# Two transformer layers on one core: units 1 and 2 transposed by DMA, room of the MLP lent to q and k, left-over projections laid by what is awaited

## The chip, the core and the metric

The kernel runs on one core of a Trainium2 chip. The core has five engines that work side by side, each through its own instructions in order: TensorE (PE, matmuls; its weight loads are listed apart as PEld), VectorE (DVE), ScalarE (ACT), GpSimd (POOL) and SyncE (SP). Here SP only issues DMAs; ACT issues the weight loads. All DMAs run on 16 DMA engines. Operands lie in SBUF with 128 partitions, matmul results in PSUM. An instruction waits on semaphores for what it needs, and everything behind it on its engine waits with it.

The metric is the device time of one execution in microseconds, lower is better. Before the change it is 1573.81 us (median of 3 runs, 1573.06 to 1575.74).

## The reference

Two layers over 2048 rows of 640 numbers. Each layer is sliding-window attention (32 heads of 20, a query sees itself and the 255 rows before it) and an MLP with a squared ReLU, both on layer-normalised rows, both added to the residual:

```python
def _A_ref(x, wqkv, wo):
    qkv = (x @ wqkv).reshape(B, S, 3, H, Dh).transpose(2, 0, 3, 1, 4)
    q, k, v = qkv[0], qkv[1], qkv[2]
    scores = jnp.einsum("bhqd,bhkd->bhqk", q, k) * (Dh ** -0.5)
    mask = (idx[:, None] - idx[None, :] >= 0) & (idx[:, None] - idx[None, :] < W)   # W = 256
    p = _softmax(jnp.where(mask, scores, -1e9))
    return jnp.einsum("bhqk,bhkd->bhqd", p, v).transpose(0, 2, 1, 3).reshape(B, S, D) @ wo

def _B_ref(x, w1, b1, w2, b2):
    r = jnp.maximum(x @ w1 + b1, 0)
    return (r * r) @ w2 + b2

x = x + _A_ref(_layernorm(x), wqkv, wo)
x = x + _B_ref(_layernorm(x), w1, b1, w2, b2)
# and both once more, with the same weights
```

## The kernel before

**Units and stages.** The work is cut into 16 units of 256 rows: eight for each layer, `u` from 0 to 15. A unit passes through these stages. Products are made from f16 pairs (a high half and the remainder as a low half) in three matmuls, so each projection below has three matmuls where the mathematics has one.

- The layernorm, then its rows transposed into `yT` (high and low halves). Units 0, 1 and 2 are transposed on TensorE (`ln_t`, which calls `split_t` at L382): ten 128x128 transposes a unit into PSUM, and from there copies on ScalarE (L389) and subtractions on VectorE (L390). Later units go through `ln_cross`: ScalarE casts a row block (L452), VectorE makes the low half (L456), and SP transposes both by DMA (L459), four transposes a unit.
- `stage_qk`: q and k, 75 matmuls each, in three pieces (two pieces of 30 and one of 15). A piece's PSUM bank is copied by ScalarE (the high half, L519) and then by VectorE (the low half, L522) into `qd`, and `leave` writes the rows to DRAM (L554, L556) and loads them back head by head (L560). Unit 0 does so piece by piece, later units after their third piece. `qd` is one buffer (`bufs=1`); k of unit 0 lies in the front half of `hraw` instead (the profile calls it `stg`), the space that later holds the MLP's `hh`.
- `stage_v`: v, 60 matmuls of 128x320, into one of six `vt` tiles.
- Attention in 8 quads a unit (four heads each). `max_quad` makes the scores once to find each row's maximum (`m`; L705 in unit 0 and 8, L673 elsewhere; VectorE reduces at L653 or L690). `max_out` turns the maxima of two quads by a transpose (`tr<-ident,mx`, L759) and `rows_out` sends them by DMA into two extra rows of q (`qt<-mT`, L727). `exp_quad` makes the scores again with the maximum subtracted (`s`; L856, L810), four exponentials on ScalarE (L795) and masks on GpSimd and VectorE; `pv_quad` multiplies by v (L901), and the result goes to DRAM (L921). The `m` of a quad runs three quads ahead of its `s` (`LEAD`). Both `m` and `s` write the same PSUM tiles `bb`, so each waits until the other's have been read.
- `load_o` fetches a unit's attention output, divides by the sums (L986, L989) and makes the pair `od` (L993, L996); `stage_o` multiplies by `wo` in two halves of 30 matmuls, adds the residual (L1025) and normalises again; `stage_y` (units 0 and 14, 15) transposes by TensorE, `y_cross` (others) by DMA; `stage_f` is the MLP, 180 matmuls into `hh` and 180 out of it.

All matmuls of projections and MLP rotate through two PSUM banks (tag `mm`), shared with `pv` and the transposes.

**What sets the order.** The program is laid out once, by a planner in the kernel's own code: `now` is its estimate of TensorE's time, and every job of another engine is posted with a cost, the jobs it depends on and an urgency (`post`, `dma`). When a job could start by `now` plus 250 ns it is put into its engine's program, the smallest number in `urgency` first. The costs decide only the order of instructions; at run time semaphores hold back what isn't ready. "Dense" work (projections, MLP) is a generator; while a quad's step waits for something by the planner's clock, the next piece of dense work is laid. `flow` does this for unit 0: its dense work is `ahead_all`, the projections of units 0, 1 and 2. What is left of it after unit 0's last quad is `rest`. `together` does it for units 1 to 15, with dense work of the unit before and the one after. For unit 1 the dense work is

```python
parts += [some(rest, left_over - 9e3), stage_o(0), some(rest, 4e3), stage_y(0, some(rest, 2e3), rest)]
```

where `some(rest, c)` lays about c ns of it. `KEEP` and `MID` say the same for the end of the program.

**Other tenants.** kts[2] (`kt_96`), the K tile of unit 2, first holds raw weights, then `yT` of unit 1 (`place`), then raw pieces of w2. `hraw` serves unit 0's k, and later `od` of unit 0 and `hh`; its second half lies idle during unit 0.

## Time and profile before

| | before |
|---|---|
| median of 3 runs | 1573.81 us |
| the profiled execution, whole | 1573.51 us |
| its span, first to last instruction | 1571.8 us |
| mean granted TensorE clock | 0.993 |
| TensorE idle after 162.57 us | 10.5 us |
| TensorE rows `tr<-ident,xt` (units 1 and 2, `y` of 0 and 14) | 40 of 286 ns each |

A row of the time view gives start and length in us, engine, source line, operation, `output<-input`, shape, and in brackets how long the engine stood idle before it and what ended that. A row of a group gives the busy time, the mean ns of one, and after the second bar the idle time before all of them. The duration of a single matmul (273 ns) holds its way through the array; in a row of them one starts every 0.11 to 0.15 us. "PEclk" is the share of full speed that TensorE's clock was granted. In the queue rows, "SPq" is a DMA issue on SP.

### The profile page before, as it was taken

The numbers are of one execution on the slowest core, as the hardware profiler recorded it, in microseconds if no ns is written. First come the engines' busy times: TensorE is split into PE (matmuls) and PEld (weight loads), VectorE is DVE, ScalarE is ACT, GpSimd is POOL, SyncE is SP. The second block draws the span as 40 slices with busy tenths as digits, with TensorE's granted clock in tenths as the row PEclk, the third lists the DMA queues.
The fourth block names the chain that finished last, engine by engine and source line by source line (L and its number), as shares of the span: only waits on it lengthen the run. The fifth ranks groups of instructions, "written<-read, shape, count | busy, mean of one in ns | idle before, by whom it ended". The sixth has DMA issues, their size and how long they took to land.

```text
span 1571.8 us, 58938 instructions
## 1 busy us (share of the span) xinstructions
PE 1541.4 (98%) x25842; PEld 1202.1 (76%) x25842; DVE 1041.4 (66%) x2248; ACT 669.1 (43%) x1369; POOL 453.6 (29%) x847
## 2 busy tenths in 40 slices
PE   8898999999999999999999999999999999999999
PEld 7565778777787877878777787877878778786777
DVE  8767775676756667666565756667676676667642
ACT  4554535345343443534434353344534434354422
POOL 1211414224141331413214142331513314132412
PEclk9999999999999999999999999999999999999999
DMA  9655244352433514354254433524344353432120
GB/s 277 173 166 151 63 124 92 91 130 60 115 97 103 115 51 125 88 120 97 72 134 81 116 97 104 113 54 123 88 126 90 71 133 74 118 89 59 30 68 18
DMA packets 243370, 160.86 MB, mean 102 GB/s; under 512 B 91176, under 2 KB 226856, under 8 KB 243112
## 3 DMA queue, kind: packets, MB, share of 16 engines
q1 hardware_dynamic: 236744, 147.58, 37.5%
q10 hardware_dynamic: 6368, 9.50, 2.1%
q8 instruction: 203, 3.33, 0.9%
q14 instruction: 55, 0.45, 0.1%
HBM read 84.68 MB, written 52.95 MB: 88 GB/s over the span
## 4 chain that ended last, share of the span: by engine, by line
PE 79%; DVE 7%; POOL 2%; issue 2%; ACT 1%; DMA 0%; SPq 0%; ACTq 0%; DVEq 0%; POOLq 0%
PE acc L339 61%; PE pv L901 6%; PE bb L810 5%; PE bb L673 4%; DVE mx L690 2%; PE bb L901 2%; POOL bmv L376 1%; POOL pt L824 1%; ACT pt L795 1%; DVE xt L378 1%; DVE bb L687 1%; DVE x L1128 0%; DVE bst L365 0%; DVE ot L916 0%; DVE bb L653 0%
## 5 line engine op out<-in xcount | busy, mean ns | idle before, releaser
L795 ACT ACTIVATE pt<-bb 128x640 f32<-128x640 f32 (+2 forms) x512 | 312.0, 684 | 210.9 <-PE bb L810 183.7
L824 POOL TENSOR_SCALAR_AFFINE_SELECT pt<-pt 64x256 f32<-64x256 f32 x448 | 195.4, 436 | 619.2 <-ACT pt L795 589.7
L339 PE MATMUL acc<-y,w_s 128*128 128x256 f16 x2880 | 328.9, 273 | 1.3 <-DVE y L390 1.2
L339 PE MATMUL acc<-w_s,hh 128*128 128x320 f16 (+1 forms) x2340 | 326.7, 297 | 0.1
L339 PEld LDWEIGHTS <-w_s 128*128 128x128 f16 x2880 | 275.5, 98 | 40.4 <-issue 2.3
L339 PEld LDWEIGHTS <-hh 128*128 128x128 f16 x2340 | 222.1, 98 | 86.8 <-issue 0.4
L690 DVE TENSOR_REDUCE mx<-bb 128x4 f32<-128x1024 f32 x224 | 274.0, 1223 | 6.2
L339 PE MATMUL acc<-yT,wq_s 128*128 128x256 f16 x2250 | 259.5, 273 | 3.5 <-DVE qd L522 2.5
L339 PEld LDWEIGHTS <-wq_s 128*128 128x128 f16 x2400 | 230.7, 98 | 41.2 <-issue 7.3
L833 DVE COPY_PREDICATED_SCALAR pt<-drop,zero 128x256 f32 x224 | 99.7, 498 | 178.9 <-ACT pt L795 178.2
L1099 DVE TENSOR_TENSOR hh<-r,hh 128x256 f16<-128x256 f32 x192 | 97.1, 519 | 112.1 <-ACT hh L1096 106.9
L901 PE MATMUL pv<-pt,vt 64*32 64x192 f32 (+5 forms) x3840 | 167.8, 304 | 0.5 <-POOL pt L867 0.3
L913 ACT COPY ot<-pv 128x256 f32<-128x256 f32 x128 | 47.6, 372 | 270.7 <-PE bb L901 244.3
L1093 POOL TENSOR_TENSOR r<-r 128x256 f32<-128x256 f32 x192 | 121.4, 652 | 136.1 <-ACT r L1089 133.4
L901 PE MATMUL bb<-pt,vt 64*32 64x64 f32 (+3 forms) x3584 | 153.9, 301 | 0.0
L901 PEld LDWEIGHTS pv<-pt,vt 64*32 64x32 f32 (+1 forms) x3840 | 126.0, 106 | 31.7 <-issue 3.7
L339 PE MATMUL acc<-wo_s,od 128*128 128x320 f16 x960 | 142.4, 303 | 5.8 <-ACT od L993 5.8
L339 PE MATMUL acc<-wq_s,yT 128*128 128x320 f16 x900 | 132.2, 302 | 1.3 <-DVE kt L390 0.5
L687 DVE COPY_PREDICATED bb<-maskq,bb 128x256 f32<-128x256 uint16 x224 | 93.8, 423 | 59.1 <-PE bb L673 56.6
L339 PEld LDWEIGHTS <-od 128*128 128x128 f16 x960 | 92.0, 99 | 45.8 <-ACT od L993 6.3
L1089 ACT ACTIVATE r<-acc,b1s 128x256 f32<-128x256 f32 x192 | 81.1, 476 | 96.0 <-PE acc L339 94.0
L901 PEld LDWEIGHTS bb<-pt,vt 64*32 64x32 f32 x3584 | 116.2, 106 | 0.4 <-DVE pt L833 0.2
(105 smaller groups left out, 1462.0 us busy)
## 6 DMA issues: line engine op xcount, KB each, us to landing
qt<-qk SPq DMA_DIRECT2D x30, 480.0 KB
kt<-qk SPq DMA_DIRECT2D x30, 480.0 KB
qk<-qd SPq DMA_DIRECT2D x17, 640.0 KB
o<-ot SPq DMA_DIRECT2D x256, 42.0 KB
od<-o SPq DMA_DIRECT2D x14, 640.0 KB
qk<-yl SPq DMA_DIRECT2D x13, 640.0 KB
qk<-qd SPq DMA_DIRECT2D x17, 320.0 KB
xt<-in_A_x_dram SPq DMA_DIRECT2D x16, 320.0 KB
```

The costliest lines, as they stand in the source:

```text
L339: nc.tensor.matmul(acc, lhs(a, c), rhs(b, c), start=(k == 0), stop=(k == 3 * nk - 1))
L673: nc.tensor.matmul(flat[e][rows, o:o + b - a], qt[r, p, i * P + 64 * h:i * P + 64 * (h + 1)], kt[r, p, a + to:b + to], start=True, stop=Tr ...
L687: nc.vector.copy_predicated(wins[:, :, 4 * Q:], later, wins[:, :, :Q])
L690: nc.vector.tensor_reduce(most, wins[:, :, Q:], axis=mybir.AxisListType.X, op=ALU.max)
L795: return lambda: nc.scalar.activation(room_of(box)[:, a:b], bank[:, a:b], AF.Exp, scale=SCALE / (QS * QS))
L810: nc.tensor.matmul(flat[e][h * Q:(h + 1) * Q, c0:c1], kt[r, 2 * qd + j, k0:k0 + Q], qt[r, 2 * qd + j, q:q + c1 - c0], start=True, stop=Tru ...
L824: nc.gpsimd.affine_select(out=m, in_=m, pattern=[[0, 4], [-1 if k else 1, Q]], base=0, fill=0.0, compare_op=ALU.is_gt if k else ALU.is_ge, ...
L833: nc.vector.copy_predicated(m, drop[:, k:k + 1, :].bitcast(mybir.dt.uint16).to_broadcast([P, 4, Q]), zero.unsqueeze(1).to_broadcast([P, 4, ...
L901: nc.tensor.matmul(pv[h][32 * jj:32 * (jj + 1), q0 * Q:(q0 + w) * Q], vf[r, c:c + 32], boxes[e]["pt"][r, a:b], start=(k == 0), stop=(k == ...
L1089: nc.scalar.activation(box["r"], acc[:, f, :], AF.Relu, bias=b1s[:, f0 + f:f0 + f + 1], scale=1.0 / (YS * WS))
L1093: nc.gpsimd.tensor_tensor(box["r"], box["r"], box["r"], op=ALU.mult)
L1099: nc.vector.tensor_sub(hh[:, 1, f, :], box["r"], hh[:, 0, f, :])
```

## The change

Four things change in the code.

1. Units 1 and 2 are transposed by DMA (`ln_early`, which calls `cross` as the later units do). The room for the casts is the second half of `hraw` ("side1").
2. k of units 0 and 1 is evicted into the front half of `hraw` ("side0"), q of unit 2 into the second ("side1"); k of unit 2 and the q of units 0 and 1 use `qd`. A record `left` keeps, for each of these buffers, which DRAM writes still read it, and the planner counts them as what the next tenant's copies depend on.
3. In unit 1 the left-over projections are laid by `until`: before `stage_o(0)` until the first two quarters of `od` are due by the planner's clock, before `stage_y` until the first block of `y` is, and between its two blocks until the second is.
4. Numbers of the planner: urgencies, the cost and landing time of the row DMAs, `KEEP` and `MID`.

```diff
-    urgency = {"out": 0, "od": 0.5, "cross": 2, "mask": 0, "turn": 1, "exp": 0.5, "ln": 1, "y": 1, "clear": 0.5}
+    urgency = {"out": 0, "od": 1, "cross": 1, "mask": 0, "turn": 1, "exp": 1, "ln": 1, "y": 0.5, "clear": 0.5}
...
+    def ln_early(u, place=None):
+
+        def dst():
+            yTs[u] = place
+            if place is None:
+                yTs[u] = sb.tile([P, 2, KC, T], F16, name="yT", tag="yT", bufs=1)
+            return yTs[u]
+
+        pre[u] = cross(lns.pop(u), dst, lambda: hraw[:, KC * T:2 * KC * T].bitcast(F16).rearrange(
+            "p (i a n) -> p i a n", i=2, a=2), 1)
+        left["side1"] = ((0, -u), pre[u], [])
...
-                if j and u == 0:
-                    qd = hraw[:, :KC * T].bitcast(F16).rearrange("p (c a n) -> p c a n", a=2, n=T)
+                if j and u < 2:
+                    qd, k = side(0), "side0"
+                elif u == 2 and not j and opened0:
+                    qd, k = side(1), "side1"
...
-                    qd = sb.tile([P, KC, 2, T], F16, name="qd", tag="qd", bufs=1)
+                    qd, k = sb.tile([P, KC, 2, T], F16, name="qd", tag="qd", bufs=1), "qd"
...
-                lo_ = post("D", 70 + 267 * n, low, post("A", 60 + 212 * n, high, wait=wait, prio=pr), prio=pr)
+                old = left.get(k, ())
+                if k and (j, u) != old[:1]:
+                    old = left[k] = ((j, u), [], old[1] if old else [])
+                hi_ = post("A", 60 + 212 * n, high, *(old[2] if k else ()), wait=wait, prio=pr)
+                lo_ = post("D", 70 + 267 * n, low, hi_, prio=pr)
...
+                if k:
+                    old[1].append(wrote)
...
-        return dma(spread, 16384, ready, n=4, cost=600.0, prio=0)
+        return dma(spread, 16384, ready, n=4, cost=650.0, prio=0, land=land)
...
+    def until(dense, jobs):
+
+        while not all(j.end is not None and j.end <= now[0] + LOOK for j in jobs()):
+            c = next(dense, None)
+            if c is None:
+                break
             yield c
...
-    QKC, VC, OC, FCST, LNC, CARRY, KEEP, MID = 16.4e3, 8.2e3, 8.2e3, 39.2e3, 1.2e3, 18e3, 28e3, 8e3
+    QKC, VC, OC, FCST, LNC, CARRY, KEEP, MID = 16.4e3, 8.2e3, 8.2e3, 39.2e3, 1.2e3, 18e3, 24e3, 10e3
...
         yield from stage_qk(0)
+        ln_early(1, place)
         yield from stage_v(0, range(2))
-        yield from ln_t(1, place)
         ln_load(2)
         yield from stage_v(0, range(2, 4))
+        ln_early(2)
         yield from stage_qk(1)
-        yield from ln_t(2)
         yield from stage_v(1)
...
-            urgency.update({"out": 0, "od": 1, "cross": 0.5, "mask": 0, "turn": 0.7, "exp": 0.5, "ln": 0.5, "y": 0.5, "clear": 0})
+            urgency.update({"out": 0, "od": 1.5, "cross": 1, "mask": 0, "turn": 0.7, "exp": 0.7, "ln": 0.5, "y": 1, "clear": 0.5})
...
-            parts += [some(rest, left_over - 9e3), stage_o(0), some(rest, 4e3), stage_y(0, some(rest, 2e3), rest)]
+            parts += [until(rest, lambda: ols[0][2][:2]), stage_o(0), until(rest, lambda: [ys[0, 0][1]]), stage_y(0, until(rest, lambda: [ys[0, 1][1]]), rest)]
```

Where the instructions stand is shown at three places; source lines differ by some 30 between the two programs, since the change adds lines.

ScalarE in the opening, from the third group of raw weights on (`kt_96`). `qd` and `stg` take q and k of unit 0 piece by piece, 128x2x256 is a piece of two, 128x256 the last. Before:

```order
L519 ACTIVATE qd<-acc 128x2x256
L271 ACTIVATE wq_s<-kt_96 128x5x128 x3
L519 ACTIVATE stg<-acc 128x2x256
L519 ACTIVATE qd<-acc 128x256
L519 ACTIVATE stg<-acc 128x256
L592 ACTIVATE vt_97<-acc 128x16x20
```

And of the changed kernel:

```order
L271 ACTIVATE wq_s<-kt_96 128x5x128 x3
L534 ACTIVATE qd<-acc 128x2x256
L534 ACTIVATE stg<-acc 128x2x256
L452 CAST stg<-xt 128x640
L300 DMA w_s<-in_A_wo_dram 32x5x640
L452 CAST stg<-xt 128x640
L534 ACTIVATE qd<-acc 128x256
L534 ACTIVATE stg<-acc 128x256
L622 ACTIVATE vt_97<-acc 128x16x20 x2
```

The weight conversions have moved ahead of q's second piece, and both casts of unit 1's rows ahead of the last pieces of q and k.

SP's queue right behind that, in the changed kernel: `kt_96<-stg` are unit 1's transposes, `yT<-stg` unit 2's, L583 and L585 the writes of q and k, L589 their loads by head, `qt<-mT` the first rows of maxima.

```order
L459 DMA_TRANSPOSE kt_96<-stg 128x5x128 x3
L589 DMA qt<-qk_0_267 60x6x256 x2
L589 DMA kt_94<-qk_1_310 60x6x256 x2
L583 DMA qk_0_267<-qd 128x512
L585 DMA qk_0_267<-qd 128x256
L583 DMA qk_1_310<-stg 128x512
L585 DMA qk_1_310<-stg 128x256
L459 DMA_TRANSPOSE kt_96<-stg 128x5x128
L430 DMA xt<-in_A_x_dram 128x640 x2
L757 DMA qt<-mT 1x8x128 x4
```

The eight transposes are new; before, the same loads and writes follow one another without them.

VectorE in unit 1 of the changed kernel, around the halves of `stage_o(0)`: `x_1539` is the residual of the first half, L1056 the addition of one `wo` bank, L365 to L370 the layernorm's statistics, L717 and L720 the reduction of a quad's maxima, L1027 the low half of a quarter of `od`, here the last.

```order
L1056 SCALAR_TENSOR_TENSOR x_1539<-acc,x_1539 128x320
L717 COPY_PREDICATED bb_143<-maskq,bb_143 128x4x64
L720 TENSOR_REDUCE mx<-bb_143 128x4
L1056 SCALAR_TENSOR_TENSOR x_1539<-acc,x_1539 128x320
L365 BN_STATS bst<-x_1539 128x6
L946 TENSOR_TENSOR ot<-bb_143,ot 128x256
L365 BN_STATS bst<-x_1539 128x6
L369 BN_AGGR bmv<-bst 128x2
L370 TENSOR_SCALAR bmv<-bmv 128x1
L1027 TENSOR_TENSOR od<-od 128x5x64
```

Before, the last quarter of `od` stands ahead of the first addition; now it stands behind both additions of the first half.

On TensorE the 20 transposes of units 1 and 2 are gone. Ahead of `stage_o(0)` all 60 v matmuls of unit 2 are laid now, and none is left for the places behind it; before, 60 of them stood between `stage_o(0)` and the MLP. Unit 0's last quad has the same projections ahead of it as before. From unit 1's seventh `m` (162.57 us in the profile of before) both orders lay the same matmuls, with a few of them moved over a neighbouring quad.

More of the change, by code (lines that the diff above doesn't have):

```diff
@@ L523, in low, with evict @@
                                                op0=ALU.mult, op1=ALU.subtract)
-            def evict(wait, n=n, c0=c0, high=high, low=low, jobs=jobs, j=j, dst=dst, qd=qd):
+            def evict(wait, k=k, n=n, c0=c0, high=high, low=low, jobs=jobs, j=j, dst=dst, qd=qd):
                 pr = urgency["out"]
-                lo_ = post("D", 70 + 267 * n, low, post("A", 60 + 212 * n, high, wait=wait, prio=pr), prio=pr)
+                old = left.get(k, ())
[3 more added lines that the diff above has]
+                lo_ = post("D", 70 + 267 * n, low, hi_, prio=pr)
                 jobs.append(lo_)
                 if u == 0:
-                    leave(u, j, dst, qd, lo_, c0, n)
+                    wrote = leave(u, j, dst, qd, lo_, c0, n)
                 elif c0 + n == KC:
-                    leave(u, j, dst, qd, lo_, 0, KC)
+                    wrote = leave(u, j, dst, qd, lo_, 0, KC)
+                else:
+                    return
+                if k:
+                    old[1].append(wrote)
             for c in range(n):
@@ L540, with side @@
     trips = {}
+    left = {}
+    opened0 = [True]
+    def side(k):
+        return hraw[:, k * KC * T:(k + 1) * KC * T].bitcast(F16).rearrange("p (c a n) -> p c a n", a=2, n=T)
     rows_of = {}
@@ L577, in leave @@
             load(*(rowset.get(u, ()) if j else ()))
+        return wrote
     def stage_v(u, which=range(4)):
@@ L719, with rows_out @@
     mxjobs = {}
-    def rows_out(qt, G, mT, ready):
+    def rows_out(qt, G, mT, ready, land=LAND):
         def spread():
@@ L941, in load_o @@
         l, g = divmod(u, NG)
+        opened0.clear()
         if late:
@@ L1179, in some @@
             yield c
+    def until(dense, jobs):
[3 more added lines that the diff above has]
+                break
+            yield c
     def portion(dense, cost):
@@ L1336 @@
             step(c)
-    left_over = 3 * (QKC + VC) + 2 * LNC - used[0]
+    left_over = 3 * (QKC + VC) - used[0]
     rate[0] = 320.0
```

7 lines of the change are left out of this document (4 added, 3 removed).

## The prediction

> **What bounds the kernel now.** I read the page first: span, busy shares and chain.
>
> ```profile
> span 1571.8 us, 58938 instructions
> PE 1541.4 (98%) x25842; PEld 1202.1 (76%) x25842; DVE 1041.4 (66%) x2248; ACT 669.1 (43%) x1369; POOL 453.6 (29%) x847
> PE 79%; DVE 7%; POOL 2%; issue 2%; ACT 1%; DMA 0%; SPq 0%; ACTq 0%; DVEq 0%; POOLq 0%
> ```
>
> TensorE is the bound: it is idle for 1571.8 - 1541.4 = 30.4 us. What an edit can win is idle time, time at the halved clock, and the few matmuls it takes away. So the second view is the busy time by stage. Columns: stretch, its length, then PE, PEld, DVE, ACT and POOL busy, granted clock, DMA share, GB/s.
>
> ```profile
> 27.87:47.70 19.83, 16.96 (x128) 11.32 (x126) 15.06 (x68) 4.22 (x10) 1.09 (x2) 0.91 0.94 224
> 47.70:112.67 64.97, 56.43 (x650) 39.55 (x650) 46.87 (x141) 37.03 (x78) 15.80 (x33) 0.96 0.61 174
> 112.67:162.57 49.90, 44.22 (x700) 31.97 (x697) 39.02 (x77) 23.48 (x47) 10.91 (x23) 0.91 0.49 130
> 162.57:1571.80 1409.23, 1398.73 (x24171) 1096.78 (x24170) 915.59 (x1905) 589.42 (x1211) 420.34 (x772) 1.00 0.38 93
> ```
>
> The stretches end where TensorE begins unit 0's v of its first half (27.87), its first scores for the exponentials (47.70), the work after its last `pv` (112.67), and unit 1's seventh maxima (162.57, from where both orders lay the same work). The first three hold 2.87 + 8.54 + 5.68 = 17.1 us of idle and, by their clocks, 1.8 + 2.6 + 4.5 = 8.9 us at half rate. The last, 1409 us long, holds 10.5 us. The change acts almost only ahead of 162.57, so **at most about 29 us** can go: 26 us, and 3 us of transposes.
>
> The third view is TensorE's rows in order of time (start, length; in brackets the idle time before and who ended it), and ScalarE's two that explain them.
>
> ```profile
> 27.87 3.29 PE L339 MATMUL acc<-wq_s,yT 128*128 128x320 f16 x23
> 32.48 0.49 PE L403 MATMUL tr<-ident,xt 128*128 128x128 f32 x3
> 36.05 4.42 PE L339 MATMUL acc<-wq_s,yT 128*128 128x320 f16 x19 [0.49 <-DVE kt L390]
> 47.70 0.49 PE L856 MATMUL bb<-qt,kt 62*128 62x256 f16 x7 [1.45 <-DMA qt<-mT]
> 66.24 3.69 PE L339 MATMUL acc<-kt,wq_s 128*128 128x256 f16 x20 [1.86 <-ACT ot L913]
> 79.37 1.25 PE L339 MATMUL acc<-wq_s,kt 128*128 128x320 f16 x8 [1.49 <-DVE yT L390]
> 109.80 0.71 PE L339 MATMUL acc<-yT,wq_s 128*128 128x256 f16 x5 [2.50 <-DVE qd L522]
> 126.36 7.04 PE L339 MATMUL acc<-wo_s,od 128*128 128x320 f16 x30 [3.81 <-ACT od L993]
> 65.32 0.60 ACT L519 ACTIVATE qd<-acc 128x512 f16<-128x512 f32 x1 [3.19 <-DMA qk<-qd]
> 108.42 0.60 ACT L519 ACTIVATE qd<-acc 128x512 f16<-128x512 f32 x1 [3.41 <-DMA qk<-qd]
> ```
>
> Three causes are to be seen: unit 2's transposes (79.37) and unit 1's (32.48 to 36.05); the single `qd` buffer, where k's first copy waits until q's rows have left (ScalarE at 65.32 and 108.42, so TensorE at 66.24, behind the same queue, and 109.80); and the attention output that isn't normalised when its projection comes (126.36).
>
> Holds cost twice. Same columns as above:
>
> ```profile
> 107.00:110.00 3.00, 0.50 (x6) 0.29 (x4) 1.20 (x4) 1.58 (x4) 0.41 (x1) 1.00 0.02 6
> 110.00:113.00 3.00, 3.00 (x61) 1.71 (x60) 2.55 (x6) 1.36 (x4) 1.90 (x3) 0.74 0.22 44
> 113.00:116.00 3.00, 3.00 (x21) 2.33 (x20) 2.97 (x5) 0.17 (x1) 0.00 (x0) 0.69 0.39 131
> 36.00:38.00 2.00, 1.95 (x9) 1.18 (x9) 2.00 (x14) 0.00 (x0) 0.00 (x0) 0.58 1.17 214
> 38.00:40.00 2.00, 2.00 (x10) 1.15 (x9) 0.87 (x6) 0.04 (x1) 0.00 (x0) 0.56 1.09 295
> ```
>
> After the 2.50 us hold the clock is 0.74 and 0.69 for 6 us, which is 1.7 us lost; after unit 1's transposes 0.58 and 0.56 for 4 us, 1.7 us again. I charge 1.7 us for each hold of 2 us and more. [...]
>
> **The change part by part: the opening, 27.87 to 47.70.** Removed are unit 1's ten transposes: between 32.48 and 36.05 TensorE spends 3.57 us, less 0.5 us for one quad's maxima: 3.1 us with their waits, and the 1.7 us of clock behind them. What comes in stands in the order on ScalarE: the copies of q's and k's last piece now stand behind both casts of unit 1's rows. (The new comparison sets a pair against a one-element tuple, so it never matches, and the planner puts each piece of unit 0 behind the last one's write.) TensorE's v of unit 0 needs the bank of q's last piece. The rows of before to lay it by:
>
> ```profile
> 24.98 0.49 DVE L365 BATCH_NORM_STATS2 bst<-xt 128x6 f32<-128x320 f32 x1
> 26.86 0.41 DVE L522 SCALAR_TENSOR_TENSOR qd<-acc,qd 128x256 f16<-128x256 f32 x1
> 30.83 0.61 DVE L378 TENSOR_SCALAR xt<-xt,bmv 128x640 f32<-128x640 f32 x1 [0.19 <-POOL bmv L376]
> L452 ACT CAST yl<-xt 128x640 f16<-128x640 f32 x52 | 38.0, 731 | 36.4 <-DVE xt L378 33.6 <-PE acc L339 2.3 <-ACT pt L795 0.5
> L456 DVE TENSOR_TENSOR yl<-xt,yl 128x640 f16<-128x640 f32 x52 | 42.6, 819 | 1.2 <-ACT yl L452 1.2
> ```
>
> Before, that bank was free at 26.86 + 0.41 = 27.3. Now the second `xt` ends at about 30.5 (its statistics, which start at 24.98 in the first row, stand one place further ahead, ahead of the third weight group), the cast (0.73) at 31.2, the piece's copy (0.4) at 31.6, the low halves behind the second L456 (0.82) at 32.2. TensorE, 0.9 us late by the conversions that moved ahead of q's second piece, stands from 28.8 to 32.2, then runs cold: 0.9 + 3.4 + 1.7 = 6.0 us against 4.8 us removed. The first scores wait for the row DMA as before (1.45 us); I lay them at 48.5 with 10 projection matmuls (1.15 us) fewer behind them: **2.0 us lost**.
>
> What TensorE no longer does, SP, ScalarE and VectorE do:
>
> ```profile
> L459 SPq DMA_TRANSPOSE yT<-yl x52: 1199/1227/2467, 192.5 to 1334.2; - x52
> L390 DVE TENSOR_TENSOR yT<-tr,yT 128x384 f16<-128x384 f32 (+1 forms) x4 | 1.9, 486 | 0.3 <-ACT yT L389 0.3
> ```
>
> Eight transposes take 8 x 1.23 = 9.8 us of SP's queue. Three of unit 1's stand ahead of the loads for quads 3 to 5, one ahead of unit 2's `xt` and of the first rows. I lay the fourth at 36.4 to 37.6 and its first reader at 43.5; a transpose lands within some 3 us, so it costs nothing while the queues keep up (if not: rival two). On VectorE four L456 replace eight L390, 3.3 against 3.7 us: nothing.
>
> **Unit 0's quads, 47.70 to 112.67.** Of 64.97 us, 8.54 are idle, 2.6 clock, 1.5 ten transposes: 52.4 us of work, now 53.5 with the 10 matmuls. k of unit 1 goes to `side0` and q of unit 2 to `side1`, both read out long before: the two `qd` waits go. What is late next is VectorE and ScalarE: VectorE's 46.87 us stand in 54 to 58 us instead of 65.
>
> ```profile
> L795 ACT ACTIVATE pt<-bb 128x640 f32<-128x640 f32 (+2 forms) x512 | 312.0, 684 | 210.9 <-PE bb L810 183.7 <-PE bb L856 15.5 <-DVE x L1128 3.5
> L690 DVE TENSOR_REDUCE mx<-bb 128x4 f32<-128x1024 f32 x224 | 274.0, 1223 | 6.2
> ```
>
> The maxima wait until ScalarE's four exponentials (0.4 to 0.7 us each) have left the banks, the next scores until VectorE's reductions (1.2 each) have. Laid quad by quad, five times the maxima stand 0.2 to 0.9 us, 2.8 us together, and a q or k copy that ScalarE puts between the exponentials takes 1.1 more: 3.9 us. So 57.4 us, to 105.9: **7.6 us won**.
>
> **Unit 1's first half, 112.67 to 162.57.** Of 49.90 us, 5.68 are idle, 4.5 clock: 39.7 us of work. The 3.81 us wait goes: with 40 q/k matmuls (0.115 us), 60 of v (3.29 / 23 = 0.143) and 3.9 us of scores and a `pv` ahead, `wo` comes 17 us after unit 0's last `pv`, and `od` was ready after 126.36 - 112.67 = 13.7. But then nothing is left: the order has no projection between `wo` and the MLP. Before, 60 of 0.14 us stood there, 8.6 us. What is late instead, laid by VectorE's order: the maxima behind the casts of `od` 1.1 us; `wo`'s second half behind both additions and the statistics 2.0; the second half's transposes behind its layernorm 2.3; the scores behind the reduction moved past it 1.4. The layernorm's price is read from before:
>
> ```profile
> 137.51 0.48 DVE L1025 SCALAR_TENSOR_TENSOR x<-acc,x 128x320 f32<-128x320 f32 x1
> 139.56 0.61 DVE L378 TENSOR_SCALAR xt<-x,bmv 128x640 f32<-128x640 f32 x1 [0.34 <-POOL bmv L376]
> ```
>
> 137.51 to 140.17 is 2.7 us, against 3 us of cover that VectorE's reductions share. Sum 6.8 us, and 1.7 for one cold stretch: 48.2, to 154.1: **1.7 us won**, more only if the chain runs through.
>
> **The rest, 1409 us:** the same matmuls. In each unit some 5 to 8 move over a quad, and one of four transposes changes place with the row maxima's: nothing, from -1 to +2 us. The other urgencies only choose that order.
>
> Sum: -2.0 + 7.6 + 1.7 = 7.3 won ahead of 162.57. The profiled execution took 1573.51 us, 0.3 below the median of 1573.81. **Forecast 1566.0** (7.3 to 7.8 won).
>
> **Rivals.** *One, the quads run through.* VectorE was busy for 72% of the second stretch, so it has room; without the 3.9 us, and with half of the 8.5 in the third, 1566 - 8 = 1558. For it: nearly no waits after 162.57 at 66%. Against: 82% here.
>
> *Two, unit 1's transposes land late.* From 36 to 40 us the DMA share is 1.17 and 1.09, and `wo`'s loads queue there.
>
> ```profile
> w_s<-in_A_wo_dram ACTq DMA_DIRECT2D x4, 400.0 KB
> ```
>
> 1.64 MB at the 214 and 295 GB/s of those rows are some 6.5 us. Were the fourth behind them, it would land at 47, not 41: 3.2 us of hold and 1.7 of clock, with the quads' waits doubled (3.9): 1575. [...]
>
> *Three, slower.* In every later unit the last transpose of `y` now stands behind the maxima's.
>
> ```profile
> 237.75 6.66 SPq L459 DMA_TRANSPOSE y<-yl  x4
> 244.96 1.13 SPq L747 DMA_TRANSPOSE mt<-mh  x1
> 252.56 4.00 PE L339 MATMUL acc<-y,w_s 128*128 128x256 f16 x35
> ```
>
> It would end at about 247.4, with 5.2 us to the MLP. If it landed later than that by 1.2 us in 13 units, 15.6 us would go: 1581.6. It decides from 0.8 us a unit on. Against it: transposes land in under 3 us.
>
> *Four, the left-over doesn't do what it is named for.* Two of the three new calls find nothing to lay; that is in the forecast at 6.8 us.
>
> **How the numbers follow.** Forecast, 1562 to 1570: 0.60. Rival one, 1555 to 1562: 0.13. Rival two, 1570.5 to 1576.5: 0.18. Rival three: 0.09. A measurement of this kernel tells about 0.2% (3.1 us) from no change, so faster is 0.73, same 0.18, slower 0.09. The range leaves out a third of rival one, a fifth of rival two and rival three: 1558 to 1575.5.
>
> **What would show it.** In the changed profile: a hold of 3 us and more ahead of the first `acc<-wq_s,yT`, ended by VectorE's `qd`; no ScalarE wait for `qk<-qd`; `wo` without a hold at its first half and holds of about 2 us at its second and at the last `tr`; the seventh maxima of unit 1 near 154. It is wrong if the first `kt,wq_s` matmul of unit 1 waits for a DMA, or if the stretch behind gains or loses over 2 us.

## The result, and the profile after

The changed kernel takes **1561.38 us** (median of 4 runs, 1560.94 to 1563.26), before 1574.57 on the same chip (1573.06 to 1575.74): a ratio of 0.9919, 95% interval 0.9902 to 0.9936. It is faster by 13 us, and the forecast was 7.8: the time lies 0.6 us below the band of 1562 to 1570 that the forecast had for itself, and in the band of rival one.

The page of the changed kernel, span and busy time:

```profile
span 1559.6 us, 58897 instructions
PE 1533.5 (98%) x25822; PEld 1198.6 (77%) x25822; DVE 1043.3 (67%) x2244; ACT 669.7 (43%) x1365; POOL 451.8 (29%) x847
```

TensorE's idle time is 1559.6 - 1533.5 = 26.1 us, 30.4 before. The same stretches as in the prediction (length, PE, PEld, DVE, ACT, POOL busy, clock, DMA share, GB/s), in the changed kernel:

```profile
28.88:48.14 19.26, 14.34 (x108) 9.19 (x107) 14.79 (x66) 3.32 (x8) 2.02 (x2) 0.91 0.86 189
48.14:104.05 55.91, 53.94 (x649) 38.69 (x650) 41.26 (x126) 34.24 (x72) 14.60 (x33) 1.00 0.87 217
104.05:152.36 48.31, 43.47 (x698) 32.29 (x696) 40.60 (x80) 25.47 (x50) 14.54 (x23) 0.93 0.57 148
152.36:1559.60 1407.24, 1396.00 (x24171) 1095.42 (x24170) 921.01 (x1910) 591.53 (x1213) 415.15 (x772) 1.00 0.38 93
```

TensorE goes on with unit 0's first scores at 48.14 (47.70 before), unit 0's last `pv` is done at 104.05 (112.67), unit 1's seventh maxima begin at 152.36 (162.57), and the rest takes 1407.24 us (1409.23). So -0.4, +9.1, +1.6 and +2.0 us: 12.2 in all.

The same 12.2 us by kind. In both profiles half clock comes in steps of 3.41 us, each worth 1.71: six before (36.3, 67.1, 111.4, two from 125.1, and 1452.9 us), three after (34.2, two from 140.1), 5.1 us. Idle time is 4.3 us less. The 2.7 us that are left are about what the twenty transposes took.

TensorE's rows of the changed kernel that answer to those of the prediction:

```profile
33.06 0.70 PE L339 MATMUL acc<-wq_s,yT 128*128 128x320 f16 x4 [4.18 <-DVE qd L537]
47.61 0.27 PE L886 MATMUL bb<-qt,kt 62*128 62x256 f16 x1 [0.36 <-DMA qt<-mT]
101.48 0.71 PE L339 MATMUL acc<-yT,wq_s 128*128 128x256 f16 x5 [0.64 <-DVE qd L537]
129.86 0.75 PE L840 MATMUL bb<-qt,kt 62*64 62x128 f16 x37 [1.34 <-DVE ot L946]
140.24 1.30 PE L403 MATMUL tr<-ident,xt 128*128 128x128 f32 x5 [1.78 <-DVE xt L378]
1441.23 0.97 PE L339 MATMUL acc<-wo_s,od 128*128 128x320 f16 x4 [1.97 <-ACT od L1024]
```

The opening hold is there (4.18 us), the waits for `qk<-qd` and the 3.81 us ahead of `wo` are gone, the chain behind `y`'s layernorm is short of cover as laid. The hold of 1.97 us near the end is the same as before, row for row.

### The profile page after: what moved, and what is told of

It reads as the page before. It is cut to its first block, busy times and chain, and to the rows that moved or that the text cites. A ratio compares the mean times of both kernels' runs of the same rounds, so it can differ in the third digit from the quotient of the medians.

```text
span 1559.6 us, 58897 instructions
## 1 busy us (share of the span) xinstructions
PE 1533.5 (98%) x25822; PEld 1198.6 (77%) x25822; DVE 1043.3 (67%) x2244; ACT 669.7 (43%) x1365; POOL 451.8 (29%) x847
## 5 line engine op out<-in xcount | busy, mean ns | idle before, releaser
L854 POOL TENSOR_SCALAR_AFFINE_SELECT pt<-pt 64x256 f32<-64x256 f32 x448 | 199.3, 445 | 582.1 <-ACT pt L825 560.0
L720 DVE TENSOR_REDUCE mx<-bb 128x4 f32<-128x1024 f32 x224 | 273.2, 1224 | 6.8
L943 ACT COPY ot<-pv 128x256 f32<-128x256 f32 x128 | 47.6, 372 | 276.1 <-PE bb L931 247.2
L931 PE MATMUL bb<-pt,vt 64*32 64x128 f32 (+3 forms) x3584 | 153.5, 301 | 0.0
L717 DVE COPY_PREDICATED bb<-maskq,bb 128x256 f32<-128x256 uint16 x224 | 93.8, 423 | 85.7 <-PE bb L703 80.0
L339 PEld LDWEIGHTS <-yT 128*128 128x128 f16 x900 | 87.1, 98 | 40.0 <-issue 6.2
```

The source lines that it names most:

```text
L339: nc.tensor.matmul(acc, lhs(a, c), rhs(b, c), start=(k == 0), stop=(k == 3 * nk - 1))
L717: nc.vector.copy_predicated(wins[:, :, 4 * Q:], later, wins[:, :, :Q])
L720: nc.vector.tensor_reduce(most, wins[:, :, Q:], axis=mybir.AxisListType.X, op=ALU.max)
L854: nc.gpsimd.affine_select(out=m, in_=m, pattern=[[0, 4], [-1 if k else 1, Q]], base=0, fill=0.0, compare_op=ALU.is_gt if k else ALU.is_ge, ...
L931: nc.tensor.matmul(pv[h][32 * jj:32 * (jj + 1), q0 * Q:(q0 + w) * Q], vf[r, c:c + 32], boxes[e]["pt"][r, a:b], start=(k == 0), stop=(k == ...
L943: nc.scalar.copy(ot[:, qd % 2], to)
```

## The experiments

Each kernel is the changed one with an edit, unless said; the two named "alone" are the kernel before with one. Runs were taken on several chips, the kernel before beside each; its median there is 1573.67 to 1574.57 us. "To unit 1's wo" is the time from the start to the first matmul of unit 1's product with `wo`, with TensorE's idle time in it (its length less TensorE's busy time) and the number of steps at half clock. Behind it all fourteen profiles take 1343 to 1349 us, and up to it 212 to 232 us, so that most of the differences arise ahead of it.

| kernel | median us | ratio to before (95%) | to unit 1's wo | idle | half-clock steps |
|---|---|---|---|---|---|
| before | 1574 | 1 | 224.3 | 19.9 | 5 |
| changed | 1561.38 | 0.9919 (0.9902 to 0.9936) | 214.1 | 14.8 | 3 |
| e0_again | 1560.22 | 0.9912 (0.9899 to 0.9925) | 212.8 | 15.8 | 2 |
| e1_compare | 1575.75 | 1.0012 (1.0002 to 1.0022) | 230.2 | 24.6 | 7 |
| e2_one_qd | 1562.30 | 0.9923 (0.9910 to 0.9935) | 215.2 | 17.9 | 3 |
| e3_turn_on_pe | 1576.57 | 1.0016 (1.0005 to 1.0026) | 230.5 | 23.9 | 7 |
| e4_some | 1569.85 | 0.9971 (0.9961 to 0.9981) | 221.2 | 21.0 | 5 |
| e5_old_numbers | 1571.87 | 0.9989 (0.9979 to 1.0000) | 223.6 | 20.9 | 7 |
| e6_blind | 1565.15 | 0.9944 (0.9927 to 0.9961) | 218.1 | 17.1 | 5 |
| f1_early_alone | 1582.75 | 1.0055 (1.0039 to 1.0071) | 231.7 | 26.8 | 7 |
| f2_rooms_alone | 1568.80 | 0.9969 (0.9957 to 0.9980) | 220.6 | 19.8 | 2 |
| e7_swap | 1561.72 | 0.9922 (0.9908 to 0.9937) | 217.7 | 17.8 | 4 |
| e8_od_first | 1558.95 | 0.9901 (0.9885 to 0.9918) | 213.2 | 16.1 | 2 |
| e9_warm | 1556.52 | 0.9887 (0.9872 to 0.9902) | 212.4 | 12.0 | 2 |

### The changed kernel again

No edit.

> The changed kernel once more, unaltered, as the mark for the others. Time 1561.4 us within 1.5. What it is to tell besides: in both first profiles TensorE stands 1.97 us ahead of the same projection of the last units (acc<-wo_s,od, ended by ScalarE's od), but only before the change 3.4 us at the halved clock follow. Theory: the halved clock comes in steps of a grid of 3.41 us (every start of such a stretch in one trace is a multiple of 3.413 us from the others), and a hold costs clock when enough of it falls into one step; where the grid lies differs from execution to execution. Then the hold of 1.97 us is there again and may or may not be followed by 3.4 us of half clock, which is 1.7 us of time either way, while the holds near 29 to 33 us and 137 to 142 us are cold again or move by a step. Rival: the end of the changed kernel is laid better; then no such stretch after 150 us in any execution of it.

Measured: 1560.22 us. The hold near the end is there, with 1.96 us, and no half clock follows. The opening hold, 4.18 us again, cost two steps here and one in the first profile; the chain behind `y` cost two there and none here, with nearly the same holds. So where half clock falls differs between executions of one program, and part of every difference below 3.4 us can be that.

In both first profiles the hold near the end is the same, and only before the change half clock follows it. The window view, the step that holds it and the step behind, before:

```profile
1449.45:1452.86 3.41, 1.45 (x44) 0.91 (x43) 2.57 (x8) 2.48 (x5) 0.93 (x3) 1.00 0.20 55
1452.86:1456.28 3.42, 3.42 (x74) 1.98 (x80) 2.85 (x6) 0.36 (x1) 1.52 (x3) 0.50 0.00 0
```

and of the changed kernel, by the grid on which its own half-clock steps lie (from 34.25 and from 140.06 us, 31 steps of 3.413 us apart):

```profile
1437.13:1440.54 3.41, 2.14 (x48) 1.26 (x46) 2.33 (x6) 1.60 (x3) 0.18 (x1) 1.00 0.19 52
1440.54:1443.96 3.42, 2.65 (x105) 1.84 (x106) 2.63 (x8) 1.24 (x3) 2.27 (x5) 1.00 0.02 3
```

Before, the whole hold lies in one step (TensorE busy 1.45 of 3.41 us) and the next step runs at 0.50. After, it is cut into 1.27 and 0.69. Twelve traces have this hold, 1.96 to 1.97 us each: in four (before, e2, e7, f2) it lies whole in one step, and half clock follows; in eight the larger part is 1.03 to 1.71 us, and it never does.

### The comparison set right

```diff
-                if k and (j, u) != old[:1]:
+                if k and (not old or (j, u) != old[0]):
```

> The comparison in the eviction of q and k set right (a pair against the recorded pair), nothing else. ScalarE's copies of unit 0's last pieces then stand ahead of the casts of unit 1's rows. Theory (the order of ScalarE is the whole cause of the 4.18 us that TensorE stands from 28.88 us on): the hold falls below 0.7 us, the half clock at 34.2 us goes, and the time falls by 4 to 5.5 us against the changed kernel, to about 1556.5. Rival (what the first scores for the exponentials wait for is the rows of the maxima, made by VectorE and a DMA, not TensorE): they start at 46.5 us or later with a hold of 1.5 us and more ahead of them, and the time falls by 1.5 us or less. A second rival: the casts, now later, make unit 1's transposed rows late, with a hold of over 1 us ahead of unit 1's first q or k matmuls.

Measured: 15.5 us slower than e0. The opening hold is gone, and another stands 19 us later. ScalarE's rows; the second has the shortest, median and longest time of one of its issues of `wo` in ns:

```profile
38.14 7.56 ACTq L300 DMA_DIRECT2D w_s<-in_A_wo_dram  x3
L300 ACTq DMA_DIRECT2D w_s<-in_A_wo_dram x4: 567/572/717, 38.1 to 49.2; - x4
45.91 0.60 ACT L534 ACTIVATE qd<-acc 128x512 f16<-128x512 f32 x1 [8.15 <-DMA w_s<-in_A_wo_dram]
51.26 0.60 ACT L534 ACTIVATE qd<-acc 128x512 f16<-128x512 f32 x1 [4.75 <-DMA xt<-in_A_x_dram]
```

and TensorE's, there and later:

```profile
51.94 0.80 PE L339 MATMUL acc<-kt,wq_s 128*128 128x256 f16 x3 [5.40 <-DVE qd L537]
139.29 0.27 PE L703 MATMUL bb<-kt,qt 60*64 60x256 f16 x1 [2.26 <-ACT pt L825]
185.50 0.75 PE L703 MATMUL bb<-kt,qt 60*64 60x128 f16 x24 [1.80 <-DMA kt<-qk]
213.01 0.37 PE L703 MATMUL bb<-kt,qt 60*64 60x256 f16 x1 [2.13 <-ACT pt L825]
```

In the new order ScalarE issues three loads of `wo` in a row, and q of unit 1 is copied behind them. The 7.56 us aren't three slow issues, since none takes over 0.72 us. The trace's semaphores tell what ScalarE waits for: the third issue (45.14) waits until the DMA that last used its semaphore has landed. That is a load of q which SP issued at 38.58, complete at 45.12, so ScalarE stands 5.3 us between the second issue (39.25 to 39.83) and the third. The DMA engines are 97% busy from 38 to 46 us; that this made the load slow fits, but wasn't tried apart. Two further weight loads, issued at 49.21 and 50.80, wait in the same way, each for a load of `xt`, and the copy at 51.26 stands behind them. Later, at 185.50, unit 2's first maxima wait for k: its load was issued at 177.62 us (161.68 in the changed kernel), because the tile holds raw pieces of `w2` until VectorE's last conversion (172.54 against 157.36). All of this comes from one comparison in the eviction: the planner's clock shifts and everything behind is laid differently. **So undoing a part in the planner doesn't price that part.** None of the expected outcomes had that size.

### One qd

```diff
-                if j and u < 2:
+                if j and u == 0:
...
-                elif u == 2 and not j and opened0:
-                    qd, k = side(1), "side1"
```

> k of unit 1 and q of unit 2 go to the one buffer qd again, all else as in the changed kernel. Theory (the single buffer's waits were what was won in unit 0's quads): ScalarE waits for the DMA of qk<-qd some 3 us twice, TensorE 1.9 and 2.5 us behind it, with up to 1.7 us of half clock for each: 4.4 to 7.8 us slower than the changed kernel. Rival (VectorE and ScalarE bind the quads anyway): the waits come back on ScalarE but TensorE's holds are covered, 2 us slower or less.

Measured: 1562.30 us, 2 us above e0 with intervals that overlap. That is the rival's size, but not its cause, as the next run shows: the planner, which now knows of the waits, lays other work there. TensorE's longest two holds there are 1.27 us at 101.19 and 1.09 us at 103.67.

### One qd, and the planner not told

As above, and

```diff
-                hi_ = post("A", 60 + 212 * n, high, *(old[2] if k else ()), wait=wait, prio=pr)
+                hi_ = post("A", 60 + 212 * n, high, *(old[2] if k and u == 0 else ()), wait=wait, prio=pr)
```

> As with one qd for k of unit 1 and q of unit 2 (1562.3 us), and besides the planner isn't told that the copies of units 1 and 2 wait for the DMA that reads the buffer, as it wasn't before the change. Theory (what replaced the waits of 1.86 and 2.50 us is that the planner knows of them and lays other work there, not the second buffer): ScalarE stands 3 us for qk<-qd again with other work behind it, TensorE 1.5 to 2.5 us at one or two places between 60 and 115 us, 2 to 6 us slower than with one qd. Rival (those waits were a consequence of the transposes on TensorE, or are covered): within 1.5 us of the run with one qd.

Each engine's order is here that of the changed kernel, only the buffers differ: this is the price of the rooms alone. Measured: 1565.15 us, 4.9 above e0, 3.8 above the first run of the changed kernel and 2.9 above one qd. ScalarE and TensorE:

```profile
102.75 0.60 ACT L532 ACTIVATE qd<-acc 128x512 f16<-128x512 f32 x1 [2.99 <-DMA qk<-qd]
```

```profile
104.12 1.22 PE L339 MATMUL acc<-yT,wq_s 128*128 128x256 f16 x5 [2.70 <-DVE qd L535]
```

2.70 us against 0.64 in the changed kernel (101.48 us there), and two half-clock steps from 103.09 us: 2.1 + 3.4 = 5.5. The theory holds, at one place of two.

### The rooms alone, on the kernel before

```diff
-                if j and u == 0:
+                if j and u < 2:
                     qd = hraw[:, :KC * T].bitcast(F16).rearrange("p (c a n) -> p c a n", a=2, n=T)
+                elif u == 2 and not j and opened0:
+                    qd = hraw[:, KC * T:2 * KC * T].bitcast(F16).rearrange("p (c a n) -> p c a n", a=2, n=T)
```

> The kernel before, with k of unit 1 and q of unit 2 in the two halves of the MLP's room and nothing else: every engine's order is that of before, only the buffers differ. Theory (the prediction's: the two waits for qk<-qd go, with their half clock): TensorE's holds of 1.86 us at 66 us and 2.50 us at 110 us go, 4.4 to 7.8 us faster than before, 1566 to 1569.5. Rival (something else is late there at once): the holds shrink, but what comes out is less than 2 us faster.

Again no instruction moves. Measured: 1568.80 us, ratio 0.9969, 5 us faster than before. The holds of 1.86 and 2.50 us are gone or down to

```profile
104.52 0.71 PE L339 MATMUL acc<-yT,wq_s 128*128 128x256 f16 x5 [0.64 <-DVE qd L524]
120.59 0.45 PE L339 MATMUL acc<-wo_s,od 128*128 128x320 f16 x2 [3.81 <-ACT od L997]
130.38 0.28 PE L762 MATMUL tr<-ident,mx 128*16 128x128 f32 x1 [2.73 <-DVE x L1029]
```

and of the gain some goes into a new hold of 2.73 us at 130.38. The two runs agree: **the rooms are worth about 5 us**, at either end of the change (4 to 5 by the one, 3 to 7 by the interval of the other).

### The transposes, undone and alone

Undone:

```diff
-        ln_early(1, place)
         yield from stage_v(0, range(2))
+        yield from ln_t(1, place)
...
-        ln_early(2)
         yield from stage_qk(1)
+        yield from ln_t(2)
```

> Units 1 and 2 are transposed on TensorE again, in their old places, all else as in the changed kernel. Twenty transposes are 2.7 us of TensorE (busy time less what half clock cost, before against after). Theory (by the steps of the prediction): in the opening the hold of 4.18 us goes, and the transposes with their waits of 0.2 to 0.7 us and one half-clock stretch come instead, 0.4 to 2 us in favour of TensorE's transposes; in the quads the transposes of unit 2 and their waits (0.8, 0.2 and 1.5 us) cost 4 us: in sum 2 to 4 us slower than the changed kernel. Rival (the transposes by DMA pay at both places): 6 us slower or more. Second rival (they pay at none): no slower.

Alone, on the kernel before: `ln_early`, the reverse of these lines, and the estimate `left_over` without the transposes' cost.

> The kernel before with the transposes of units 1 and 2 by DMA alone: no buffers, no record, no new rule, no new numbers. Theory (the transposes carry the gain, as the undoing of them cost 15 us and that of the buffers 1 to 2): the twenty transposes (2.7 us), their holds (3.9 us) and their half clock (1.7 us) go, 5 to 8 us faster than before, 1566 to 1569, with the qk<-qd waits still there. Rival (the parts only work together, since each alone shifts the planner's order and w2's conversions): within 3 us of before or slower, and unit 2's k is loaded after 166 us.

Measured: undone 16 us slower than e0, alone 9 us slower than before. Both theories fall: undone, the first rival's 6 us and more came, and alone, the rival. Undone, TensorE's transposes stand for VectorE:

```profile
40.37 0.77 PE L403 MATMUL tr<-ident,xt 128*128 128x128 f32 x5 [3.20 <-DVE kt L390]
81.18 1.30 PE L403 MATMUL tr<-ident,xt 128*128 128x128 f32 x5 [3.77 <-DVE xt L378]
```

Alone, other holds come:

```profile
51.04 0.37 PE L867 MATMUL bb<-qt,kt 62*128 62x256 f16 x1 [3.00 <-DVE bst L365]
66.64 0.60 PE L339 MATMUL acc<-kt,wq_s 128*128 128x256 f16 x4 [3.32 <-DVE qd L533]
194.55 0.75 PE L684 MATMUL bb<-kt,qt 60*64 60x128 f16 x20 [2.65 <-DMA kt<-qk]
```

Unit 2's k is loaded at 168.3 us undone and at 185.9 us alone. The edit's own price can't be read from either run, since the whole order behind it differs: what the transposes alone are worth isn't shown.

### Left-over by amounts

```diff
-            parts += [until(rest, lambda: ols[0][2][:2]), stage_o(0), until(rest, lambda: [ys[0, 0][1]]), stage_y(0, until(rest, lambda: [ys[0, 1][1]]), rest)]
+            parts += [some(rest, left_over - 9e3), stage_o(0), some(rest, 4e3), stage_y(0, some(rest, 2e3), rest)]
```

> The left-over projections of unit 1 are laid by amounts again (9 us kept back ahead of the first product with wo, 4 us and 2 us behind it), all else as in the changed kernel. Theory (the prediction's step): the product with wo stands some 3.8 us for od again, with up to 3.4 us of half clock, and in exchange the holds behind y's layernorm (1.34, 0.64, 1.78 and 0.36 us, with 3.4 to 6.8 us of half clock) become shorter: within 2 us of the changed kernel, 1559 to 1563. Rival (the new rule is where unit 1's first half was won): 4 us slower or more. Second rival, from the two runs that were 15 us slower: whatever leaves projections behind the first wo moves the conversions of w2 back, so that the load of unit 2's k (kt<-qk, issued at 161.7 us in the changed kernel, 177.6 and 168.3 us in those two) comes after 166 us, and 6 to 15 us go behind 150 us.

Measured: 9.6 us slower than e0: the first rival. Nearly all of it lies ahead of the first `wo` (124.69 us, 123.39 in e0): up to there TensorE has been idle for 17.2 us (11.0 in e0), with four steps at half clock (two in e0). (Unit 2's k is loaded at 166.65 us, and nothing waits for it.) Up to 108 us the order is that of the changed kernel, so this place can be read. Groups of TensorE's matmuls from 108 to 125 us here (count, busy time, mean, idle time before):

```profile
L703 PE MATMUL bb<-kt,qt 60*64 60x64 f16 (+3 forms) x76 | 3.2, 305 | 4.9 <-ACT pt L825 4.9
L840 PE MATMUL bb<-qt,kt 62*64 62x64 f16 (+3 forms) x76 | 1.7, 222 | 2.1 <-DVE mx L720 2.1
L339 PE MATMUL acc<-wo_s,od 128*128 128x320 f16 x2 | 0.5, 342 | 0.0
L339 PE MATMUL acc<-yT,wq_s 128*128 128x256 f16 x1 | 0.3, 273 | 0.0
```

and from 106 to 122.5 us in the changed kernel:

```profile
L339 PE MATMUL acc<-wq_s,yT 128*128 128x320 f16 x60 | 8.8, 299 | 0.3 <-DVE mT L795 0.3
L339 PE MATMUL acc<-yT,wq_s 128*128 128x256 f16 x24 | 2.8, 273 | 0.0
L703 PE MATMUL bb<-kt,qt 60*64 60x64 f16 (+3 forms) x76 | 1.8, 222 | 0.0
```

The expected hold ahead of `wo` doesn't come back as such. While `od` isn't due, the planner may not pass `stage_o`, so it lays quads with one projection matmul between them (the two of `wo` come at the end) where the changed kernel has 84. A bare quad waits about 2 us for ScalarE's exponentials, and once more for VectorE. That is 7 us of idle time in 17 us.

### The old numbers

Both sets of urgencies, cost and landing of the row DMAs, `KEEP` and `MID` as before.

> All of the planner's numbers of before (both sets of urgencies, cost and landing of the row DMAs, KEEP and MID) with the other three parts of the change. Theory (the prediction's: the numbers choose an order and are worth nothing by themselves): within 2.5 us of the changed kernel, 1559 to 1564, with the same holds in the opening (4 us) and a few tenths in unit 0's quads. Rival (the numbers were fitted to the new transposes, and without them the order falls into that of the two slow runs): unit 2's k is loaded after 166 us and the time is 5 us slower or more.

Measured: 11.7 us slower than e0, and the output is wrong in this order; why isn't known, so this is the time of an order that can't be used. Again bare quads (holds of 1.71, 1.74 and 2.26 us at 124.73, 128.06 and 147.40), four half-clock steps from 124.2 us, the first `wo` at 133.15 and unit 2's k at 172.16. The theory falls: the numbers are part of the order that pays, and with the other three parts in place even the result hangs on them. Which of them matters wasn't tried.

### One place re-ordered

To price the opening hold with the later order kept, the casts, the second block's layernorm step and the transposes of unit 1 are put back in the program until the low half of k's last piece stands:

```diff
+                if u == 0 and j and c0 + n == KC:
+                    kept[0] = False
+                    while behind:
+                        behind.pop(0)()
...
-            j = post("A", 615, high, ready, j, prio=prio)
+            j = post("A", 615, keep(high), ready, j, prio=prio)
```

> The changed kernel with one place re-ordered and every other instruction where it was: both casts of unit 1's rows, the second block's last layernorm step, their low halves and the first three transposes stand behind the copies of q's and k's last piece (unit 0), on ScalarE, VectorE and SP. All later order is that of the changed kernel, so that this is the price of that place alone, which the run with the corrected comparison couldn't tell. Theory (the prediction's: the place costs its hold and the half clock behind it): TensorE's 4.18 us from 28.9 us fall to about 1 us, the half clock at 32 to 34 us goes, 4 to 6 us faster than the changed kernel, about 1556. Rival (the rows of the maxima are late next): a hold of 2 us or more ahead of the first scores for the exponentials, ended by the DMA qt<-mT, and less than 1.5 us faster. Second rival (the transposes of unit 1, now some 2 to 4 us later, are late): a hold of 1 us or more ahead of the first kt,wq_s, and no faster.

Measured: 1561.72 us, no faster than e0. The first rival:

```profile
30.24 0.70 PE L339 MATMUL acc<-wq_s,yT 128*128 128x320 f16 x4 [1.32 <-DVE qd L544]
49.38 0.37 PE L897 MATMUL bb<-qt,kt 62*128 62x256 f16 x1 [4.69 <-DMA qt<-mT]
```

The hold falls from 4.18 to 1.32 us, and TensorE waits 4.69 us for the maxima's rows. VectorE has them ready 2.6 us sooner (40.15 against 42.71), but SP's queue is behind:

```profile
41.04 1.05 SPq L430 DMA_DIRECT2D xt<-in_A_x_dram  x2
42.19 2.90 SPq L768 DMA_DIRECT2D qt<-mT  x4
```

The rows are issued at 42.19 as in the changed kernel (42.42), now right behind the loads of `xt`, and land at 49.4 instead of 47.6. SP's queue is thus the second bound in this order. In part that is the edit's own doing: it also moves the three transposes behind SP's loads by head, and SP then issues without a pause from 31.02 to 42.09, where in the changed kernel it stands free from 40.31 to 42.42. Whether another order could have the hold's time wasn't tried; that the loads of `xt` delay the rows' landing fits, but wasn't tried apart either.

### Near the end: od's last quarter first

```diff
+            if u == NU - 2 and i == 3:
+                def times(times=times, high=high, low=low):
+                    times()
+                    high()
+                    low()
```

(and the two later jobs do nothing; every other instruction keeps its place.)

> The changed kernel with one place re-ordered near its end and all else where it was: in unit 14 ScalarE casts the last quarter of od ahead of three exponentials that stand waiting for their scores, and VectorE makes its low half ahead of the next addition. In every execution profiled so far TensorE stands 1.97 us there, and in four of eleven 3.4 us of half clock follow. Theory: the hold was only the order (the quarter's product was ready 2.5 us before the cast), so it falls below 0.3 us, no half clock can follow, and 2 us go for certain and up to 3.7: 1557.5 to 1559.5, against 1560.2 and 1561.4 of the changed kernel. Rival (VectorE or the exponentials are late next): the hold moves to the scores or to the second half's layernorm and less than 1 us comes out.

Measured: 1558.95 us, 1.3 below e0 and 2.4 below the first run. The 1.97 us are gone, and instead stand

```profile
1438.08 0.27 PE L703 MATMUL bb<-kt,qt 60*64 60x256 f16 x1 [0.42 <-ACT pt L825]
1439.27 0.75 PE L703 MATMUL bb<-kt,qt 60*64 60x256 f16 x37 [0.93 <-ACT pt L825]
1444.91 0.75 PE L840 MATMUL bb<-qt,kt 62*64 62x128 f16 x37 [0.53 <-DVE mx L720]
```

The first two are new and the third was 0.32 us: 1.97 + 0.32 - 1.88 = 0.4 us won. The rival is right on the hold. What comes besides is, by an estimate from the fourteen traces, that half clock is no longer to be expected: however the grid lies, at most 1.35 us of idle time fall into one step there, and the least after which half clock followed a step at full clock in any of them was 1.42 us. (The twelve profiles ahead of this run had it in four; the expectation says eleven.)

### TensorE kept busy in the opening hold

As e8, and

```diff
         yield from stage_qk(0)
+        for k in range(14):
+            nc.tensor.matmul(bb6[0][:, 2, :P], ident, ident, start=True, stop=True)
```

> As the run before (the last quarter of od first), and besides fourteen multiplications of the identity with itself into an idle bank stand on TensorE between unit 0's q and k and its v, 3.5 us of work that nothing reads, in the hold of 4.18 us. Theory (a hold costs clock by the idle share of one step of 3.41 us): TensorE's idle time there falls below 1 us, the half clock at 32 to 34 us does not come, v and all behind it run 1.7 to 3.4 us sooner, and as the rows of the maxima follow from TensorE's own maxima there, most of it comes out: 1 to 3 us faster than the run before. Rival (as with the swapped order: SP's queue and the rows are bound there): TensorE is sooner at the scores but waits there for the DMA qt<-mT, and the time is within 0.7 us of the run before.

Measured: **1556.52 us**, ratio 0.9887 (0.9872 to 0.9902), the fastest of all, 2.4 below e8.

```profile
28.56 3.29 PE L1364 MATMUL bb<-ident 128*128 128x128 f32 x28
32.90 0.70 PE L339 MATMUL acc<-wq_s,yT 128*128 128x320 f16 x4 [1.05 <-DVE qd L537]
45.67 0.90 PE L886 MATMUL bb<-qt,kt 62*128 62x256 f16 x8 [0.21 <-DMA qt<-mT]
```

v begins at 32.90 as in e0 and e8, at full clock, and the first scores come at 45.67 with 0.21 us of wait (48.60 in e0, 48.78 in e8). The theory holds at this place: the half clock behind the hold is gone (granted clock 1.00 from 28 to 46 us, 0.91 in the first profile of the changed kernel) and the hold's own time is not, and 3.1 us are won against e8, whose profile has two half-clock steps from 32.35. However the grid lies, at most 1.05 us of idle time fall into one step of this hold now. Further on the two profiles don't tell as much: at unit 1's `wo` 0.8 us are left, since this one has two half-clock steps from 138.38 that e8's lacks, and another 1.6 us lie behind, where the order is the same and no cause is shown. The 2.4 us rest on the medians (four runs each, which don't overlap).

## Why the prediction was right, and where it was short

**What bounds it.** Right: TensorE's idle time and half clock ahead of unit 1's `wo` explain the differences between the fourteen profiles up to there, but for 2 us to either side once the transposes and the filling are taken off; the part behind 162.57 us kept its length within 2 us (1407.24 against 1409.23). The measured time lies in rival one's band, and its mechanism carries only part of that, as the terms below show. Rival three (slower in every later unit) didn't come, rival two (late transposes of unit 1) neither: the fourth is issued at 37.99, and their first reader starts at 44.90 without a wait.

**The opening.** Place, cause and size as laid: VectorE ends a hold from 28.9 us (4.18 us, laid 3.4), one or two cold steps follow, first scores at 48.14 (laid 48.5). But the step made the order on ScalarE the loss, and the swapped order won nothing, since there SP's queue is as late. Of the 6.0 us charged there, what a run has won back is the half clock, by e9.

**The sum counted the ten projection matmuls twice.** The 1.15 us stand in the opening's 2.0 us and again in unit 0's 53.5 us of work. By the positions that the prediction laid itself (154.1 against 162.57) 8.5 us were won, not 7.3. This is 1.2 us of the shortfall.

**Unit 0's quads.** Laid 7.6, measured 9.1. The mechanism is shown (the rooms, 5 us, by two runs that move no instruction). The mis-sized term is the 3.9 us of waits for VectorE and ScalarE: TensorE's holds there add up to 1.97 us (55.91 - 53.94). This is rival one's direction, at a fifth of its way. The other 4 us of the 9.1 the prediction gave to unit 2's transposes and their waits; no run prices them with the order kept.

**Unit 1's first half.** Laid 1.7, measured 1.6: 4.8 us idle and 3.4 of half clock, 8.3 in all, laid 6.8 and 1.7. That the sums agree is luck: the same stretch of e0 (104.91 to 150.77) has 5.3 us idle and no half clock, which is 4.0 us won. That `until` finds nothing to lay two times out of three is right; what the prediction didn't see is how much the first call is worth, since it compared with a wait and not with the bare quads of e4 (9.6 us).

**The rest.** Laid 0, measured 2.0. One half-clock step, 1.7 us, is the hold near the end that fell into one step before and into two after; it is luck and no work of the change. The step "1.7 us for each hold of 2 us and more" is wrong in that: 1.97 us cost 1.7 or nothing, by where the grid lies.

Together: 7.3 laid, and 1.2 (counted twice), 0.4 (opening), 1.5 (quads), 2.0 (rest), less 0.1 (unit 1): 12.2. Numbers for the parts, each without the others, can't be added: undone in the planner, the rooms, the transposes, `until` and the numbers cost 2.1, 16.4, 9.6 and 11.7 us, 40 in all, where the change as a whole won 13; and the comparison set right, which undoes nothing, cost 15.5.

## What to carry to other kernels

Where a planner lays the order, an edit that is undone moves everything behind it; to price one place, keep the order and move only that place's instructions, or change only the buffer. A hold may be free while the clock behind it isn't (in the opening, 2.9 us less of hold won nothing in e7, and filling the hold won 3.1 us in e9 against e8): ask whether the next bound comes at the same time, and if so, fill the hold. Before a wait is laid as dead time, ask what the planner puts there, since bare attention quads can cost more than the wait (7 us idle in e4, where the wait before the change was 3.81).

## What was not expected of the hardware

In the trace of before, stretches at half clock begin at 36.33, 67.05, 111.42, 125.08 and 1452.86 us, the later ones 9, 22, 26 and 415 times 3.413 us behind the first; each is one such step long, that at 125.08 two. In the first trace of the changed kernel they begin at 34.25 and 140.06, 31 steps apart, and from the start of the span this grid lies 2.08 us off the other. In the hold that twelve traces share, 1.96 us idle within one step brought half clock each time and 1.71 us never. It is no clean bound: in the opening of the first profile 1.95 us in the step from 27.42 (TensorE busy 1.46 of 3.41 us) were followed by a step at full clock. Over all steps at full clock in the fourteen traces, from 14 us on, half clock followed each of the 33 with 1.96 us idle or more, eight of the 13 with 1.72 to 1.95 us, and of those with less only one (1.42 us, before, the step from 32.92). Behind a step at half clock 0.39 us idle in it were once enough for another (e2, the step from 141.88). What else counts stays open.

A DMA issue held its engine for another engine's DMA: in e1 ScalarE's third load of `wo` waited 5.3 us for a load of q that SP had issued 6.6 us earlier with the same semaphore, where the issues themselves took 0.57 to 0.72 us.
